# A recurrent attention and its MLP on one core: chunk gates on VectorE, a second chunk of exponents on TensorE, paired weight tails, three early blocks and a planner that knows of a shared port

## The chip, the cores and the metric

The kernel runs on one core of a Trainium2 chip. The metric is device microseconds of one execution. The core has TensorE (PE; its weight loads are shown as PEld), VectorE (DVE), ScalarE (ACT), GpSimd (POOL) and SyncE (SP), whose queue issues the DMAs. Each engine works through its own instructions in order.

## The reference, cut to what matters

Two stages follow each other. The first is an mLSTM: for 4 batches and 8 heads, over 768 steps, with head size 40:

```
m_new = max(f[t] + m, i[t])
C = exp(f[t] + m - m_new) * C + exp(i[t] - m_new) * outer(v[t], k[t])
n = exp(f[t] + m - m_new) * n + exp(i[t] - m_new) * k[t]
y[t] = sigmoid(o[t]) * (C q[t]) / max(|n.q[t]|, 1)
```

The 3072 rows of 320 values then go through an MLP: `h = x @ w_in` (320 by 2048), `g = h * erf(softplus(h))`, `out = g @ w_out` (2048 by 320). The weights arrive as 64-bit floats.

## The kernel before, in words

**Attention.** The recurrence is computed in 6 chunks of 128 steps (`NC`), for 4 batches, so there are 24 attention steps; step `s` is chunk `s // 4`, batch `s % 4`. Within a chunk all heads are done as masked matrix products: `S` (L581) multiplies k and q, `w` (L596) multiplies that with the decay matrix `dm`, `ph` (L614 to L623) forms outputs and the state's update, `sk` and `sa` (L633 to L648) keep the state, `yg`, `y` and `yy` (L654 to L668) finish a row, `tr` (L674) turns it, and `xh`, `xl` (L688, L692) store it in a high and a low part for the MLP.

**Decays.** `dm` is an exponent of cumulative gate sums with a causal mask. In chunk 0 TensorE forms the argument (`pe`, L523 to L526) from sums split into three bf16 parts, with the mask added by a product; `ex` (L535) takes the exponent from PSUM. In chunks 1 to 5 the row sums are read back from DRAM as a broadcast over all partitions (`bq`, L543, 512 KB), GpSimd adds the column part (`add`, L555), ScalarE takes the exponent (L559), and GpSimd applies the mask (`sel`, L564). The gate sums of chunk 0 are made alone (`gload` to `split`, L370 to L402). Those of all chunks are then made in one set of instructions over 768 columns on 32 partitions (`lload` to `lrest`, L416 to L450), partly on VectorE (two scans, L422 and L445) and partly on GpSimd (L428 to L437, L450), and written to DRAM (L459).

**Weights.** Twenty-two pieces of raw 64-bit weights (`win`, `tail`, `wout`) are loaded and decoded in the kernel by `decode` (L699): `val` on ScalarE (L707), `dec`, two instructions on VectorE (L712, L713), `hi` on ScalarE (L718) and `lo` on GpSimd or VectorE (L724). The last 64 rows of w_in, the tail, are loaded twice per quarter of the columns so that the high part stands in one half of the partitions and the low part in the other.

**MLP.** Two attention steps make a block of 256 rows; there are 12 blocks. A phase is half a block's MLP: `up` (L807, 64 matmuls a phase), a copy `hb` (L816 on ScalarE or L818 on VectorE), softplus `sp` (L826), `er` (L830), `mu` (L834), `gh` and `gl`, the high and low parts (L839, L844), and `dn` (L869 to L872). Softplus, erf and exp each need a table load on ScalarE.

**Order.** `Plan` (L51) orders everything. Each step is a part with an engine, a cost in microseconds, predecessors, buffers from counted slots and, for some, a due time (`target`). `issue` places parts one by one at the earliest possible time and prefers the one that is due first, shifted by a hand-kept table (`NUDGE`). The engines' queues come out of that plan. `CHAIN` fixes the order of exponents, softplus and erf on ScalarE. `ORDER` (L264) fixes the order of the phases: first halves of blocks 0 and 1, then their second halves, and then block after block. First halves need half of w_in and half of w_out. From step `CLUSTER` on, `tr`, `S` and `ph` of three steps are merged into one TensorE part. `SLOTS` and `CAPS` count buffers.

Of the kernel before, what the change touches and what calls it, by code (L numbers as in the profile page):

```python
# [9 lines left out]
F32 = mybir.dt.float32  # L10
# [8 lines left out]
L = 128  # L19
# [10 lines left out]
NB = 2  # L30
# [20 lines left out]
class Plan:  # L51
# [13 lines left out]
    def add(self, engine, cost, fn, after=(), new=(), use=(), target=None, kb=0.0, table=None, mode=0, order=()):  # L65
# [8 lines left out]
        p.into, p.leaves = None, mode  # L74
        self.parts.append(p)
        return p
# [18 lines left out]
    def issue(self):  # L95
# [34 lines left out]
        table, mode, dma = None, 0, 0.0  # L130
# [3 lines left out]
        def can(p):  # L134
            t = max(free[p.engine], p.ready)
            for b in p.new:
                for tag in b.tags:
                    s = slots[tag]
                    need = sum(tag in x.tags for x in p.new) + (KEEP.get(b.tag, 0) if tag == 'big' else 0)
                    if len(s) < need:  # L140
                        return None
                    t = max(t, sorted(s)[need - 1][0])
            return t + 2 * self.TABLE * (p.table is not None and len(p.table) > 1 and table not in p.table)

        while len(out) < len(parts):
            best = None
            for e, rs in ready.items():
                ts = [(t, p) for p in rs if (t := can(p)) is not None]
                if not ts:
                    continue  # L150
                first = min(t for t, _ in ts)
                cost = lambda p: PREFER * self.ENTER.get((mode, p.mode), 0.0) if e == 'PE' else 0.0
                _, _, t, p = min((p.late + cost(p), p.n, t, p) for t, p in ts if t <= first + 0.02)
# [13 lines left out]
            free[p.engine] = end  # L167
            if p.engine == 'SP':
# [832 lines left out]
```

## Time and profile before

| | |
|---|---|
| median of 3 runs | 493.35 us (491.83 to 493.83) |
| the profiled execution's own time | 493.03 us |
| its span, first to last instruction | 491.2 us |
| busy: PE, DVE, ACT, POOL | 449.3, 344.1, 332.6, 175.3 us |
| mean granted TensorE clock | 0.961 |
| moved by DMA | 53.75 MB |

A page of the profile gives the span in 40 slices, a digit for each engine's busy tenths, and the clock that TensorE was granted (`PEclk`). Other views of the same trace are the busy time of each engine in stretches that one chooses, the waits (who waited for whom: total, times, longest), groups of instructions by line (count, then busy total and mean ns of one, then idle time before them), a timeline (start, length, engine, line) and the chain of waits that ended last (start, length, what). Busy time of VectorE and GpSimd includes time in which an instruction has started and cannot go on.

### The profile page before, as it was taken

What the parts mean: (1) busy time and instruction counts of PE and PEld (TensorE: products, weight loads), DVE (VectorE), ACT (ScalarE), POOL (GpSimd) and SP (SyncE); (2) the same over time, 40 slices, a digit from 0 to 9 for tenths busy, and PEclk for the clock granted to TensorE, in tenths of its full rate; (3) what the DMA queues carried; (4) which work ended last, traced back from release to release, by engine and by line L of the source; (5) the groups of instructions that cost most, each with busy time, mean ns of one, the idle gap of its engine ahead of it and who ended that gap; (6) DMA issues with size and microseconds to landing.
All of it is one profiled execution on the core that took longest, in us unless ns stands there. A gap on an engine that the chain in (4) does not pass through costs nothing.

```text
span 491.2 us, 13646 instructions
## 1 busy us (share of the span) xinstructions
PE 449.3 (91%) x6013; PEld 433.4 (88%) x6013; DVE 344.1 (70%) x493; ACT 332.6 (68%) x383; POOL 175.3 (36%) x150
## 2 busy tenths in 40 slices
PE   1696863997999999999999999999999999999997
PEld 0476852986999999999999999999999999999997
DVE  2779798999849458659849658767766854755561
ACT  3554888487775569958967847757668667366691
POOL 6439476657537134223303503403403510200000
PEclk9967988798899999999999999999999999999999
DMA  8978858430553325314505314323333300000000
GB/s 245 239 243 252 259 162 259 136 90 11 152 150 95 103 65 161 109 32 136 166 4 160 120 48 136 119 77 107 119 116 85 102 3 28 1 28 2 1 27 29
DMA packets 31164, 53.75 MB, mean 109 GB/s; under 512 B 3200, under 2 KB 19840, under 8 KB 31104
## 3 DMA queue, kind: packets, MB, share of 16 engines
q1 hardware_dynamic: 31104, 52.87, 36.9%
q8 instruction: 47, 0.77, 0.7%
q14 instruction: 13, 0.11, 0.1%
HBM read 48.73 MB, written 4.13 MB: 108 GB/s over the span
## 4 chain that ended last, share of the span: by engine, by line
PE 76%; DMA 10%; DVE 8%; ACT 3%; issue 2%; POOL 1%; SPq 1%; DVEq 0%; ACTq 0%; POOLq 0%
PE h L807 32%; PE po L869 11%; PE po L872 11%; PE po L870 11%; DMA raw<-in_w_in_dram 4%; PE pa L581 4%; PE pa L614 3%; DMA raw<-in_w_out_dram 3%; DVE bits L713 3%; PE pa L618 2%; DMA dq<-dec_dr 2%; PE pa L674 1%; DVE bits L712 1%; DVE gl L844 1%; PE pa L623 1%
## 5 line engine op out<-in xcount | busy, mean ns | idle before, releaser
L807 PE MATMUL h<-xh,wh 128*128 128x256 f32 x576 | 158.3, 285 | 1.3 <-DVE hb L818 0.9
L807 PE MATMUL h<-xl,wh 128*128 128x256 f32 x576 | 157.5, 283 | 1.6 <-DVE xl L692 1.6
L869 PE MATMUL po<-woh,gh 128*128 128x320 f32 x384 | 118.7, 321 | 9.6 <-ACT o_sb L890 8.1
L870 PE MATMUL po<-wol,gh 128*128 128x320 f32 x384 | 116.2, 314 | 1.7 <-POOL wol L724 1.7
L807 PEld LDWEIGHTS h<-xh,wh 128*128 128x128 f32 x576 | 109.6, 190 | 2.3 <-DVE hb L818 1.4
L807 PEld LDWEIGHTS h<-xl,wh 128*128 128x128 f32 x576 | 109.7, 190 | 1.8 <-DVE xl L692 1.8
L807 PE MATMUL h<-xh,wl 128*128 128x256 f32 x384 | 109.1, 284 | 2.2 <-POOL wl L724 2.2
L662 POOL TENSOR_TENSOR kvo<-kvo,den 128x320 f32<-128x320 f32 x24 | 25.3, 1052 | 179.4 <-DVE kvo L658 179.4
L818 DVE COPY hb<-h 128x512 f32<-128x512 f32 x84 | 57.6, 686 | 41.4 <-PE h L807 40.8
L826 ACT ACTIVATE e<-hb 128x1024 f32<-128x1024 f32 x48 | 50.6, 1059 | 52.6 <-DVE hb L818 52.4
L869 PEld LDWEIGHTS po<-woh,gh 128*128 128x128 f32 x384 | 74.0, 193 | 11.1 <-ACT o_sb L890 8.3
L870 PEld LDWEIGHTS po<-wol,gh 128*128 128x128 f32 x384 | 74.1, 193 | 1.9 <-POOL wol L724 1.9
L834 DVE TENSOR_TENSOR hb<-e,hb 128x1024 f32<-128x1024 f32 x48 | 65.4, 1372 | 14.6 <-ACT e L830 14.6
L807 PEld LDWEIGHTS h<-xh,wl 128*128 128x128 f32 x384 | 73.1, 190 | 2.4 <-POOL wl L724 2.4
L872 PE MATMUL po<-woh,gl 128*128 128x320 f32 x384 | 73.3, 313 | 1.3 <-DVE gl L844 1.3
L844 DVE TENSOR_TENSOR gl<-hb,gh 128x1024 fp32r<-128x1024 f32 x44 | 63.1, 1435 | 5.5 <-ACT gh L839 5.1
L839 ACT ACTIVATE gh<-hb 128x1024 fp32r<-128x1024 f32 x48 | 50.3, 1054 | 20.2 <-DVE hb L834 19.9
L872 PEld LDWEIGHTS po<-woh,gl 128*128 128x128 f32 x384 | 61.5, 192 | 1.6 <-DVE gl L844 1.5
L555 POOL TENSOR_TENSOR dm<-dm,aT 128x1024 f32<-128x1024 f32 x20 | 48.2, 2409 | 18.3 <-DMA dm<-cum_dr 18.3
L830 ACT ACTIVATE e<-e 128x1024 f32<-128x1024 f32 x48 | 49.3, 1054 | 0.3
L654 DVE TENSOR_SCALAR den<-pa 128x8 f32<-128x8 f32 x24 | 3.9, 165 | 55.2 <-PE pa L623 41.8
L826 ACT ACT_TABLE_LOAD x28 | 35.9, 1283 | 4.1 <-DVE hb L818 3.6
(91 smaller groups left out, 646.3 us busy)
## 6 DMA issues: line engine op xcount, KB each, us to landing
dm<-cum_dr SPq DMA_DIRECT2D x20, 512.0 KB
qk<-in_qk_dram SPq DMA_DIRECT2D x24, 416.0 KB
kvo<-in_kvo_dram SPq DMA_DIRECT2D x24, 324.0 KB
raw<-in_w_in_dram SPq DMA_DIRECT2D x8, 512.0 KB
kvo<-in_kvo_dram SPq DMA_DIRECT2D x24, 160.0 KB
out_dram<-o_sb SPq DMA_DIRECT2D x24, 160.0 KB
raw<-in_w_out_dram SPq DMA_DIRECT2D x8, 320.0 KB
dq<-dec_dr SPq DMA_DIRECT2D x20, 128.0 KB
```

The source lines that it names most:

```text
L555: nc.gpsimd.tensor_tensor(v.dm, v.dm, aT[:, c - 1, 8 * b:8 * b + 8].unsqueeze(2).to_broadcast([128, H, L]), op=ALU.add)
L662: nc.gpsimd.tensor_tensor(v.y[:, 0:DM].rearrange("p (h d) -> p h d", d=D), v.th.rearrange("p (h d) -> p h d", d=D), v.den.unsqueeze(2).to_ ...
L807: nc.tensor.matmul(V.h[i][:, n % 2 * T:(n % 2 + 1) * T], w, m, start=(q == 0), stop=(q == len(ops) - 1))
L818: nc.vector.tensor_copy(V.hb[:, i * 512:(i + 1) * 512], V.h[i])
L826: nc.scalar.activation(V.e, V.hb, AF.Softplus)
L830: nc.scalar.activation(V.e, V.e, AF.Erf)
L834: nc.vector.tensor_tensor(V.hb, V.e, V.hb, op=ALU.mult)
L839: nc.scalar.activation(V.gh, V.hb, AF.Copy)
L844: (nc.gpsimd if f in GL_POOL else nc.vector).tensor_tensor(V.gl, V.hb, V.gh.bitcast(F32), op=ALU.subtract)
L869: nc.tensor.matmul(K.po[b], V.gh[:, ts], woh[:, w], start=start, stop=False)
L870: nc.tensor.matmul(K.po[b], V.gh[:, ts], wol[:, w], start=False, stop=False)
L872: nc.tensor.matmul(K.po[b], V.gl[:, ts], woh[:, w], start=False, stop=stop)
```

## The change

The diff is long, since the planner's tables (`CHAIN`, `NUDGE`, the sets that choose an engine) are replaced as a whole. Its parts:

- **Second chunk by TensorE.** `pe`, `rows` and the two `ex` are used for chunks 0 and 1 (`if c < 2`); `bq`, `add` and `sel` remain for chunks 2 to 5.
- **Gate sums per chunk.** `gate_chunk(c)` takes the place of both sets of gate instructions. All sums are on VectorE; the maximum is carried from chunk to chunk; sums go to DRAM in four small writes a chunk. `late`, `lg`, `lones`, `lrest` are gone.
- **Tails in pairs.** One `val` and one `dec` serve two quarters of the columns; each quarter keeps its `hi` and `lo`.
- **Three early blocks.** `EARLY = 3`, so the phases begin (0,0), (1,0), (2,0), (0,1), (1,1), (2,1).
- **The shared port in the plan.** Parts with `lock`, and all of GpSimd's, are placed one after another on a common `port` time. The costs of many parts are set anew (`add` from 2.7 to 1.95, `sel` from 1.4 to 1.15, `gl` on GpSimd from 2.8 to 2.42).
- **Engine choices.** `GL_POOL` is empty, so every `gl` is on VectorE. `y` and `yy` of steps 0 and 1 go to VectorE. `hb` of phase 4 goes from ScalarE to VectorE. `vg` of steps 1 and 3 goes to VectorE, that of step 4 to GpSimd. `lo` is on VectorE for i31, o5, o8, o9 in place of o1, o6, t0. `hi` is on VectorE for i01 and o5. `lo` of i01 is formed by two TensorE products and a ScalarE copy; `LO_PE` also lists t0, t2 and t3, but `weights_tail` no longer calls `decode`, where that set is looked up.
- **Buffers.** `dm`, `xh`, `xl`, the outputs and chunk 0's constants move into the common slots (`big`, 19 to 26).
- **Loads.** The q and k loads of steps 13 and later follow the issue of all w_out loads (`AFTER`).

```
-    def add(self, engine, cost, fn, after=(), ..., mode=0, order=()):
+    def add(self, engine, cost, fn, after=(), ..., mode=0, order=(), lock=False):
+        p.into, p.leaves, p.lock = None, mode, lock or engine == 'POOL'
...
+                    t = max(at, p.ready, port if p.lock else 0.0)
...
+            if p.lock:
+                port = end
...
+SLOTS = dict(pa=4, h=2, po0=1, po1=1, big=26, vg=2, dq=2, bits=2, den=2, gt=1, m_c=2, x0=2, aT=2, spl=1)
+EARLY = 3
+HB_ACT = {0, 6}
+HI_DVE = {'i01', 'o5'}
+LO_DVE = {'i31', 'o5', 'o8', 'o9'}
+LO_PE = {'i01', 't0', 't2', 't3'}
+GL_POOL = set()
+CLUSTER = 9
+AFTER = 13
+VG_POOL = {0, 2, 4, 6, 7}
+Y_DVE = {0, 1}
+ORDER = [(k, hh) for hh in range(2) for k in range(EARLY)] + [(k, hh) for k in range(EARLY, NK) for hh in range(2)]
...
+        @make(f'sum{c}', 'DVE', 1.05, after=[scan], new=[x0b], use=[gtb, m_b], lock=True)
+        def total():
+            v.x = x = new(sb, [128, 3, L], F32, "x0")
+            nc.vector.tensor_tensor(x[:, Y], v.gt[:, 1], v.m[:, 0:L], op=ALU.add)
+            nc.vector.tensor_tensor(x[:, Y], x[:, Y], v.m[:, 1:L + 1], op=ALU.subtract)
+            if c == 0:
+                nc.vector.memset(x[:, Y, 0:1], 0.0)
+            nc.vector.tensor_tensor_scan(out=x[:, C], data0=x[:, Y], data1=zero.to_broadcast([128, L]), initial=0.0,
+                                         op0=ALU.add, op1=ALU.add)
...
+        def kept(name, t, i, after):
+            @make(f'{name}{c}', 'SP', 1.4, kb=16.0, after=after, use=[x0b])
+            def put():
+                for b in range(B):
+                    nc.sync.dma_start(t[c, b], v.x[32 * b:32 * b + H, i])
...
-        if c == 0:
+        if c < 2:
             peb = [Buf('pa') for _ in range(2)]
...
+            def rest():
+                v.lo = new(ps, [128, 512], F32, "pa")
+                nc.tensor.matmul(v.lo, ident, v.val, start=True, stop=False)
+                nc.tensor.matmul(v.lo, minus, hi(), start=False, stop=True)
...
+        for v_ in step[AFTER:]:
+            v_.load.order.append(load)
```

More of the change, by code (lines that the diff above doesn't have):

```diff
@@ L63, in __init__, with add @@
         self.parts, self.slots = [], dict(slots)
-    def add(self, engine, cost, fn, after=(), new=(), use=(), target=None, kb=0.0, table=None, mode=0, order=()):
+    def add(self, engine, cost, fn, after=(), new=(), use=(), target=None, kb=0.0, table=None, mode=0, order=(), lock=False):
         p = Part()
@@ L129, in issue @@
         free = {e: 0.0 for e in self.LAG}
-        table, mode, dma = None, 0, 0.0
+        table, mode, dma, port = None, 0, 0.0, 0.0
         ready = {e: [p for p in parts if p.engine == e and not p.wait] for e in self.LAG}
         out = []
-        def can(p):
-            t = max(free[p.engine], p.ready)
+        for p in parts:
+            p.needs = {}
             for b in p.new:
                 for tag in b.tags:
-                    s = slots[tag]
                     need = sum(tag in x.tags for x in p.new) + (KEEP.get(b.tag, 0) if tag == 'big' else 0)
[L140 to L143, printed above, removed]
+                    p.needs[tag] = max(need, p.needs.get(tag, 0))
+            p.needs = [(slots[tag], need) for tag, need in p.needs.items()]
+            p.slow = p.table is not None and len(p.table) > 1
         while len(out) < len(parts):
@@ L385, in total @@
-    @make('sum', 'DVE', 0.6, after=[g, p_small], use=[firstb])
-    def total():
-        nc.vector.tensor_tensor_scan(out=first.x[:, 1], data0=first.y, data1=zero.to_broadcast([128, L]), initial=0.0,
-                                     op0=ALU.add, op1=ALU.add)
-    @make('rest', 'POOL', 0.9, after=[total], use=[firstb])
-    def rest():
-        x = first.x[:, 0]
-        nc.gpsimd.tensor_tensor(x, first.gt[:, 0], first.m[:, 1:L + 1], op=ALU.subtract)
-        nc.gpsimd.tensor_tensor(x, x, first.x[:, 1], op=ALU.subtract)
@@ L396, in split @@
-    @make('split', 'DVE', 2.1, after=[rest, p_cst], use=[firstb])
-    def split():
-        x, spl = first.x, first.spl
-        for m in (nm1, nm2):
-            nc.vector.tensor_copy(spl, x)
-            nc.vector.scalar_tensor_tensor(out=x, in0=spl, scalar=m, in1=x, op0=ALU.mult, op1=ALU.add)
-        nc.vector.tensor_scalar(out=spl, in0=x, scalar1=pm, scalar2=pa, op0=ALU.mult, op1=ALU.add)
-    late = SimpleNamespace()
-    R = B * H
-    gib, gfb, gmb, gyb, gcb = (Buf('late') for _ in range(5))
@@ L408, in row @@
-    def row(name):
-        return big(name)[0:R]
-    @make('lload', 'SP', 1.2, kb=200.0, new=[gib, gfb])
-    def lload():
-        late.i, late.f = row("late"), row("late")
-        for b in range(B):
-            for t, x in ((late.i, 0), (late.f, 1)):
-                nc.sync.dma_start(t[8 * b:8 * b + 8, 0:S], gates[32 * b:32 * b + 8, x])
-    @make('lscan', 'DVE', 3.2, after=[lload, p_small], new=[gmb], use=[gib, gfb])
-    def lscan():
-        late.m = row("late")
-        nc.vector.tensor_copy(late.m[:, 0:1], m0[0:R])
-        nc.vector.tensor_tensor_scan(out=late.m[:, 1:S + 1], data0=late.f[:, 0:S], data1=late.i[:, 0:S], initial=m0[0:R],
-                                     op0=ALU.add, op1=ALU.max)
@@ L440, in tile_mlstm_moe @@
-    p_lones = reset(gyb)
-    @make('lsum', 'DVE', 3.2, after=[lg, p_lones], new=[gcb], use=[gfb, gyb])
-    def lsum():
-        late.c = row("late")
-        nc.vector.tensor_tensor_scan(out=late.c[:, 0:S], data0=late.one[:, 0:S], data1=late.f[:, 0:S], initial=0.0,
-                                     op0=ALU.mult, op1=ALU.add)
-    @make('lrest', 'POOL', 2.0, after=[lsum], use=[gib, gcb])
-    def lrest():
-        nc.gpsimd.tensor_tensor(late.i[:, 0:S], late.i[:, 0:S], late.c[:, 0:S], op=ALU.subtract)
@@ L452, in gexp @@
-    @make('gexp', 'ACT', 0.85, after=[lsum], use=[gcb, gfb], table=('exp',))
-    def gexp():
-        nc.scalar.activation(late.f[:, 0:S], late.c[:, 0:S], AF.Exp)
-    def kept(name, t, src, after, buf):
-        @make(name, 'SP', 0.5, kb=100.0, after=after, use=[buf])
-        def put():
-            nc.sync.dma_start(t.rearrange("c b h l -> (b h) c l"), src()[:, 0:S].rearrange("p (c l) -> p c l", l=L))
-        return put
-    p_cum = kept('cumw', cum_dr, lambda: late.c, [lsum], gcb)
-    p_dec = kept('decw', dec_dr, lambda: late.f, [gexp], gfb)
@@ L506, in loadv, with dqp @@
             v.y = n[:, 0:DM + 64]
+        if c > 0:
+            @make(f'dq{s}', 'SP', 0.9, after=[G.dec], kb=208.0, new=[dqb])
+            def dqp():
+                v.dq = new(sb, [128, NPR, L], F32, "dq")
+                for j in range(2):
+                    n = 64 if j == 0 else D
+                    nc.sync.dma_start(v.dq[64 * j:64 * j + n],
+                                      dec_dr[c, b:b + 1].rearrange("o (p j) l -> o j p l", j=2)[:, j].to_broadcast([n, NPR, L]))
         ex, sel = [], []
-        if c == 0:
+        if c < 2:
             peb = [Buf('pa') for _ in range(2)]
-            @make(f'rows{s}', 'POOL', 0.5, after=[split, p_zeros], use=[firstb])
+            @make(f'rows{s}', 'POOL', 0.45, after=[G.split, p_zeros], use=[G.splb, earlyb], order=prev.pe if c else [])
             def rowsp():
-                nc.gpsimd.tensor_copy(splB[b][rows], first.spl[rows])
-            @make(f'pe{s}', 'PE', 1.35, after=[rowsp, p_ones, p_mask], new=peb, use=[maskb], target=due - 14, mode=3,
+                nc.gpsimd.tensor_copy(early.spl[b][rows], G.spl[rows])
+            @make(f'pe{s}', 'PE', 1.45, after=[rowsp, p_ones, p_mask], new=peb, use=[maskb, earlyb], target=due - 14, mode=3,
                   order=[step[s - 1].S] if s > 0 else [])
@@ L560, in attention @@
             ex.append(e)
-            @make(f'sel{s}', 'POOL', 1.4, after=[e], use=[dmb])
+            @make(f'sel{s}', 'POOL', 1.15, after=[e], use=[dmb])
             def sl():
@@ L585, in attention @@
         if not last:
-            @make(f'vg{s}', *(('POOL', 1.0) if s in VG_POOL else ('DVE', 0.47)), after=[*sel, loadv], new=[vgb], use=[dmb, kvb])
+            @make(f'vg{s}', *(('POOL', 0.8) if s in VG_POOL else ('DVE', 0.52)), after=[*sel, loadv], new=[vgb], use=[dmb, kvb], lock=True)
             def vgp():
@@ L707, in val @@
             nc.scalar.activation(v.val, raw().bitcast(F32)[:, :, 1], AF.Prelu, scale=REBIAS, alpha=NEGATIVE)
-        @make(f'dec{name}', 'DVE', 1.4, after=[val], use=[vb, rawb])
+        @make(f'dec{name}', 'DVE', 1.18, after=[val], use=[vb, rawb], lock=True)
         def bits():
@@ L742, in weights_in, with weights_tail @@
         win[part].append(decode(f'i{part}{k}', lambda: pair(v.raw), b, [load], lambda: wh[:, k, cs], lambda: wl[:, k, cs]))
-    def weights_tail(part):
+    def weights_tail(pair_):
         v = SimpleNamespace()
-        b = Buf('raw')
-        @make(f'tail{part}', 'SP', 1.0, kb=512.0, new=[b])
+        b, vb = Buf('raw'), Buf('bits')
+        cols = [slice(part * 512, (part + 1) * 512) for part in (2 * pair_, 2 * pair_ + 1)]
+        at = [slice(0, 64), slice(64, 128)]
+        @make(f'tail{pair_}', 'SP', 1.0, kb=512.0, new=[b])
         def load():
@@ L751, in load, with val, bits, high @@
             for i in range(2):
-                nc.sync.dma_start(v.raw[64 * i:64 * i + 64], w_in.bitcast(I32)[256:320, part * 1024:(part + 1) * 1024])
-        cs = slice(part * 512, (part + 1) * 512)
-        win[part].append(decode(f't{part}', lambda: pair(v.raw), b, [load], lambda: wh[:, 2, cs], None))
+                nc.sync.dma_start(v.raw[at[i]], w_in.bitcast(I32)[256:320, 2 * cols[i].start:2 * cols[i].stop])
+        @make(f'valt{pair_}', 'ACT', 0.7, after=[load], new=[vb], use=[b], table=('exp', 'er'))
+        def val():
+            v.val = new(sb, [128, 512], F32, "bits")
+            nc.scalar.activation(v.val, pair(v.raw).bitcast(F32)[:, :, 1], AF.Prelu, scale=REBIAS, alpha=NEGATIVE)
+        @make(f'dect{pair_}', 'DVE', 1.18, after=[val], use=[vb, b], lock=True)
+        def bits():
+            t = v.val.bitcast(I32)
+            nc.vector.tensor_scalar(out=t, in0=t, scalar1=3, scalar2=None, op0=ALU.logical_shift_left)
+            nc.vector.scalar_tensor_tensor(out=t, in0=pair(v.raw)[:, :, 0], scalar=29, in1=t,
+                                           op0=ALU.logical_shift_right, op1=ALU.bitwise_or)
+        for i in range(2):
+            name = f't{2 * pair_ + i}'
+            engine = 'DVE' if name in LO_DVE else 'POOL'
+            @make(f'hi{name}', *(('DVE', 0.36) if name in HI_DVE else ('ACT', 0.64)), after=[bits], use=[vb], lock=name in HI_DVE)
+            def high(i=i, on_dve=name in HI_DVE):
+                w = wh[at[i], 2, cols[i]]
+                if on_dve:
+                    nc.vector.tensor_copy(w, v.val[at[i]])
+                else:
+                    nc.scalar.activation(w, v.val[at[i]], AF.Copy)
+            @make(f'lo{name}', engine, dict(DVE=0.72, POOL=1.3)[engine], after=[high], use=[vb], lock=True)
+            def low(i=i, e=nc.vector if engine == 'DVE' else nc.gpsimd):
+                e.tensor_tensor(wh[at[1 - i], 2, cols[i]], v.val[at[i]], wh.bitcast(F32)[at[i], 2, cols[i]], op=ALU.subtract)
+            win[2 * pair_ + i].append(low)
     def weights_out(u):
@@ L839, in ghp @@
                 nc.scalar.activation(V.gh, V.hb, AF.Copy)
-            @make(f'gl{f}', *(('POOL', 2.8) if f in GL_POOL else ('DVE', 1.24)), after=[ghp], new=[gl], use=[hb, gh])
+            @make(f'gl{f}', *(('POOL', 2.42) if f in GL_POOL else ('DVE', 1.25)), after=[ghp], new=[gl], use=[hb, gh], lock=True)
             def glp(V=V):
```

260 lines of the change are left out of this document (143 added, 117 removed), and 102 rows, old and new, of tables (CHAIN, NUDGE).

## The prediction

> **What bounds the kernel now.** I read the 40 slices first, then busy time by stages, then TensorE's waits, then the instructions inside the bad stages.
>
> ```profile
> PE   1696863997999999999999999999999999999997
> PEclk9967988798899999999999999999999999999999
> ```
>
> From slice 12 on TensorE has no gap and a full clock; what can be won lies in the first 11 slices (12.28 us each) and the end of the last. Stages cut at the first matmul (10.30), the first `up` matmul (35.65), the middle of the decode (92) and the point where `ph` and `S` of steps 6 and 7 end the ramp (135.4). The columns are the stage and its length, then busy time and instructions of PE, PEld, DVE, ACT and POOL, then granted clock, DMA share and GB/s:
>
> ```profile
> 0.00:10.30 10.30, 0.00 (x0) 0.00 (x0) 3.03 (x8) 3.52 (x5) 7.02 (x26) 1.00 0.77 220
> 10.30:35.65 25.35, 19.96 (x406) 14.21 (x406) 16.80 (x31) 13.30 (x28) 10.49 (x14) 0.80 0.89 243
> 35.65:92.00 56.35, 37.84 (x325) 35.69 (x325) 50.17 (x56) 39.15 (x54) 38.88 (x24) 0.82 0.77 231
> 92.00:135.40 43.40, 38.87 (x640) 36.96 (x639) 39.94 (x53) 31.44 (x38) 26.56 (x19) 0.92 0.31 88
> 135.40:442.00 306.60, 306.60 (x4306) 300.75 (x4305) 210.93 (x324) 215.37 (x230) 92.31 (x69) 1.00 0.31 91
> 442.00:491.20 49.20, 46.08 (x344) 45.81 (x342) 23.18 (x25) 29.83 (x31) 0.00 (x0) 1.00 0.04 15
> ```
>
> TensorE idles 10.3, 5.4 (25.35 less 19.96), 18.5, 4.5, 0 and 3.1 us in these six stages. The 3.1 are the last copy and store. Busy time at a low clock adds an estimated 20% of 19.96, 18% of 37.84 and 8% of 38.87: 4.0 + 6.8 + 3.1 = 13.9 us. So 491.2 is about 435 us of TensorE work at full clock and 56 us lost, of which some 33 us (18.5 + 4.5 + 6.8 + 3.1) lie between 35.65 and 135.4. There VectorE is busy 89% and then 92%, more than ScalarE and GpSimd. What TensorE waits for in that stretch:
>
> ```profile
> PE po L869 <- ACT o_sb L890: 8.1, 1, 8.1
> PE pa L581 <- DVE dm L596: 2.9, 1, 2.9
> PE h L807 <- POOL wl L724: 2.2, 1, 2.2
> PE pa L618 <- DVE dm L596: 1.8, 1, 1.8
> ```
> ```profile
> 85.75 0.64 PE L869 MATMUL po<-woh,gh 128*128 128x320 f32 x1 [8.12 <-ACT o_sb L890]
> ```
>
> One wait of 8.1, and small ones behind VectorE and GpSimd that sum, with the rest of the 23.0, to 14.9. The 8.1 carries ScalarE's name, but the second fence, a row of TensorE's timeline, puts it at 77.6 to 85.75, after both early first halves of `up` and one early `dn`: TensorE has nothing else to do, since the second halves want weights still being decoded. Why are VectorE and GpSimd so late?
>
> ```profile
> 88.92 0.69 DVE L713 SCALAR_TENSOR_TENSOR bits<-raw,bits 128x512 int32<-128x512 int32 x1
> ...
> 90.13 0.42 DVE L712 TENSOR_SCALAR bits<-bits 128x512 int32<-128x512 int32 x1
> 90.58 1.66 DVE L713 SCALAR_TENSOR_TENSOR bits<-raw,bits 128x512 int32<-128x512 int32 x1
> ...
> 92.76 1.21 DVE L844 TENSOR_TENSOR gl<-hb,gh 128x1024 fp32r<-128x1024 f32 x1
> ```
> ```profile
> 90.41 1.27 POOL L724 TENSOR_TENSOR wl<-bits,wh 128x512 fp32r<-128x512 f32 x1 [1.82 <-ACT wh L718]
> ```
>
> The same L713 takes 0.69 alone and 1.66 when GpSimd's L724 runs from 90.41 to 91.68: it ends at 92.24, 0.56 after GpSimd. The two do not share, one waits out the other. The price up to 125 us:
>
> ```profile
> L713 DVE SCALAR_TENSOR_TENSOR bits<-raw,bits 128x512 int32<-128x512 int32 x22 | 26.5, 1205 | 0.8
> L712 DVE TENSOR_SCALAR bits<-bits 128x512 int32<-128x512 int32 x22 | 16.5, 752 | 6.6 <-ACT bits L707 6.6
> L818 DVE COPY hb<-h 128x512 f32<-128x512 f32 x12 | 8.2, 683 | 2.3 <-PE h L807 2.3
> L844 DVE TENSOR_TENSOR gl<-hb,gh 128x1024 fp32r<-128x1024 f32 x4 | 8.1, 2032 | 0.0
> ```
>
> Against 22 x 0.69, 22 x 0.42 and 4 x 1.21 that is 11.3 + 7.3 + 3.3 = 21.9 us of waiting counted as VectorE's busy time. **The ramp is bound by VectorE and GpSimd taking turns.**
>
> **The change, part by part.** The rows of GpSimd's work that goes, up to 125 us:
>
> ```profile
> L555 POOL TENSOR_TENSOR dm<-dm,aT 128x1024 f32<-128x1024 f32 x4 | 8.8, 2211 | 0.0
> ...
> L844 POOL TENSOR_TENSOR gl<-hb,gh 128x1024 fp32r<-128x1024 f32 x2 | 5.2, 2590 | 0.0
> ...
> L564 POOL TENSOR_SCALAR_AFFINE_SELECT dm<-dm 128x1024 f32<-128x1024 f32 x3 | 3.5, 1180 | 7.5 <-ACT dm L559 7.5
> ...
> L428 POOL TENSOR_TENSOR late<-late 32x768 f32<-32x768 f32 x1 | 1.9, 1890 | 0.1
> L429 POOL TENSOR_TENSOR late<-late 32x768 f32<-32x768 f32 x1 | 1.9, 1872 | 0.1
> ```
>
> (1) *GpSimd's relief.* Chunk 1's `add` and `sel` go (8.8 + 3.5), the late gate sums (1.9 + 1.9, and L430 and L450 over the same shape, taken as 3.3 together), and `gl` of the early phases (5.2): 24.6 us of the 65.4 that GpSimd is busy between 35.65 and 135.4, or 38%. `y` of two steps and two of the lows (`i31`, `o5`/`o8`/`o9` in place of `o1`/`o6`/`t0`) move off too, four `rows` of chunk 1 come on; these I let cancel. SP's queue loses chunk 1's four broadcasts (`bq`), the eight row loads of the late gates and four of the eight tail loads; it gains 36 small writes of chunk sums, most of them after 100 us. None of these issues is among TensorE's waits above.
>
> (2) *VectorE's account.* It gains `gl` (2 x 1.21 early), a second `split` (below, the first begins at 7.68 and the matmul behind it at 10.30, so under 2.6; I take 2.1), the sums of chunks 0 to 3, and `hb` of one phase. A gate chunk is two scans (0.48 and 0.42) and four two-input sums of 128x128 that no row shows: between nothing and the 0.42 of a scan of that size; I take 0.25, so 1.9 a chunk, 7.6 for four. The old 768-wide scans go:
>
> ```profile
> L422 DVE TENSOR_TENSOR_SCAN late<-late,m 32x768 f32<-32x768 f32 x1 | 2.9, 2904 | 0.0
> ```
>
> The paired tails keep their highs and lows and drop two `val` and two `dec`, which saves 2 x (0.42 + 0.69) = 2.2 here. In all about +2.4 + 2.1 + 7.6 + 2.7 (four `hb` like L818's 0.68) - 2.9 - 2.2 = +9.7 clean, and 38% of 21.9 = -8.3 of waiting. VectorE's busy time in the ramp hardly falls. What improves is its order and what TensorE has in hand meanwhile.
>
> (3) *The start.*
>
> ```profile
> 5.97 0.42 DVE L387 TENSOR_TENSOR_SCAN late<-late,zero 128x128 f32<-128x128 f32 x1 [2.00 <-POOL late L383]
> 7.68 0.29 DVE L400 CAST late<-late 128x256 bf16<-128x256 f32 x1 [1.29 <-POOL late L394]
> ```
>
> Two hand-overs to GpSimd (3.3 us of waiting) become four sums on VectorE itself (1.0): up to 2.3 us earlier. The first `up` also waits for DMA (89% busy from 10.30 to 35.65), so I take -1, with 0 and -2 as bounds.
>
> (4) *Third early block.* One more phase of `up`, 64 matmuls, needs only the first half of w_in and is ready in the place of the 8.1 wait. Two pieces of the chain of waits show what such matmuls take, after a wait (0.20 each) and late in the span at full clock (0.12 each):
>
> ```profile
> 45.40 6.13 PE h L807 x30
> ```
> ```profile
> 455.59 7.59 PE h L807 x64
> ```
>
> 7.6 us would nearly fill it. But block 2 needs steps 4 and 5, so I take -6.5 (bounds 0 and -8.1). The second halves and half of w_out are wanted a phase later.
>
> (5) *The other waits* (14.9): GpSimd's 38%, and an order that knows of the turns: -6.5 (0 to -12).
>
> (6) *Clock.* The slow stretches follow the waits: of 6.8 + 3.1 about half, -4.5 (0 to -8).
> The Trainium skill (TensorE: Matmul & The Clock Gate, "What's actually happening") gives about 3.4 us of idleness before the clock falls. By that only the wait of 8.1 costs clock, about 1.7 us, and the sum would come out 2.8 us higher. The trace disagrees: the slow stretch at 45.40 comes after a wait of 2.2 us.
>
> (7) *TensorE's added work.* The exponents of four steps, 4 x what one takes now:
>
> ```profile
> 14.07 0.39 PE L523 MATMUL pa<-rhsE,splB 128*128 128x512 bf16 x1
> 14.30 0.39 PE L525 MATMUL pa<-splB,rhsE 128*128 128x128 bf16 x4
> ```
>
> A step issues six such groups, 0.23 apart (14.07 to 14.30): 1.4, and 5.6 for four. The low part of `i01` is two f32 matmuls over 512 columns that no row shows: from twice the 0.23 of a bf16 one over 512 to four times that, 0.5 to 1.8; I take 1.0. Of 6.6 I put half on the path, +3 (0 if all of it falls into waits, +6.6 if none does).
>
> (8) *The steady stretch* stays at nothing: VectorE works 210.93 of 306.60 there, GpSimd 92.31, and the new chunk sums add 1.9 per four steps. Covered by that slack; without it, the second rival.
>
> Sum: -1 - 6.5 - 6.5 - 4.5 + 3 = -15.5, so 491.2 becomes 475.7. The profiled execution took 493.03, 1.83 over its span, and lies 0.3 below the median of 493.35. Predicted: 475.7 + 1.8 = 477.5.
>
> **The rivals.** *VectorE stays the bound.* By (2) its work does not shrink; 89% and 92% leave no room. Then the third block gives half its worth, the small waits and the clock stay: -1 - 3 - 1 - 1 + 2 = -4, some 489. For it: the ledger. Against: work that the first halves don't need is put off.
>
> *Slower: late chunk sums.* Before, one set of instructions made all later sums. Now each of chunks 2 to 5 goes through scans on VectorE's in-order queue, a write, a read, `add`, exp, `sel`; behind the write's wait on the one DMA queue stand the next loads of q, k and v. One broadcast took this long:
>
> ```profile
> 53.77 9.02 DMA dq<-dec_dr
> ```
>
> 1.9 + 9 + 2.2 for `add` and 1.2 for `sel` (the means of their rows) are 14.3, with the exponent some 15 us a chunk. If the order leaves half of it uncovered, 4 x 7.5 = 30 is lost: 477.5 + 30 = 507. From 3.9 uncovered a chunk the gain is gone. Against it: a full TensorE phase of cover, and the slack in (8).
>
> *TensorE never starves after the first `up`.* All of 18.5 + 4.5 + 9.9 and the start's 2 won, 6.6 paid: -28, so 465. For it: GpSimd's relief and the put-off decodes together exceed the waits. Against: a queue order planned from costs has left 23 us of waits in this trace.
>
> *The change does nothing:* the order that comes out trades one wait for another, 493.
>
> **How the numbers follow.** Forecast (471 to 484) 0.55, VectorE bound 0.16, never starves 0.16, nothing 0.05, late sums 0.08. A measurement of this kernel can tell about 0.5%, 2.5 us. Faster: 0.55 + 0.16 + 0.12 of the VectorE case = 0.83; same: 0.04 + 0.04 = 0.08; slower 0.09 (0.08 and 0.01 of the nothing case). The range takes in the VectorE case and most of the third rival: 465 to 490.
>
> **What would show it.** First matmul near 8.5 instead of 10.30; no wait of 8 us around 80, `up` of block 2 in its place; L713's line nearer to 0.9 than to 1.2 us; `add` 16 times instead of 20; TensorE without a gap from 115 to 125 on instead of 122. Wrong: VectorE over 90% busy with the waits unchanged, or waits on `dm` or `aT` at chunk borders after 150 us.

## The result, and the profile after

The changed kernel takes 481.69 us (median of four runs, 481.31 to 489.12) against 493.59 for the kernel before beside it; the ratio is 0.9761 with a 95% interval of 0.9727 to 0.9795. The run of 489.12, with a mean clock of 0.972, is not in the ratio. The profiled execution took 481.77, with a span of 480.1 and a clock of 0.989. The forecast was 477.5 (465 to 490).

The engines' busy time and two of the 40-slice strips:

```profile
PE 448.1 (93%) x6057; PEld 430.9 (90%) x6063; DVE 333.4 (69%) x550; ACT 331.7 (69%) x388; POOL 119.1 (25%) x121
...
PE   2695988999798999999999999999999999999997
...
PEclk9999998999999999999999999999999999999999
```

Before, slices 4 to 7 had 6, 8, 6 and 3 tenths of TensorE's work; now they have 5, 9, 8 and 8, and slices 11 and 13 have small dents. The clock falls below 0.9 in one slice only. GpSimd fell from 175.3 to 119.1 us. Stages cut at the first matmul, the first `up`, and then 92, 145 and 434 (columns as in the prediction's table):

```profile
0.00:8.77 8.77, 0.00 (x1) 0.01 (x1) 4.15 (x13) 3.95 (x6) 4.40 (x17) 1.00 0.73 220
8.77:29.97 21.20, 17.34 (x391) 11.96 (x393) 13.40 (x30) 12.32 (x26) 6.51 (x8) 0.92 1.01 301
29.97:92.00 62.03, 50.85 (x708) 47.08 (x703) 50.65 (x94) 43.21 (x66) 25.67 (x25) 0.94 0.68 200
92.00:145.00 53.00, 50.27 (x643) 48.31 (x644) 41.93 (x63) 46.48 (x52) 11.94 (x10) 1.00 0.20 57
145.00:434.00 289.00, 286.77 (x4012) 280.90 (x4013) 203.57 (x332) 197.43 (x214) 70.58 (x63) 1.00 0.30 92
434.00:480.10 46.10, 42.90 (x316) 42.63 (x314) 19.67 (x21) 28.35 (x28) 0.00 (x0) 0.99 0.04 15
```

TensorE idles 8.8, 3.9, 11.2, 2.7, 2.2 and 3.2 us: 32.0 in all, 41.9 before. Busy time at a low clock is 17.34 x 0.08 + 50.85 x 0.06 = 4.4 us, 13.9 before. What is left, 443.7, is work at full clock, 435.4 before. So the span fell by 11.1 = 9.9 (idle) + 9.5 (clock) - 8.3 (more work). VectorE is busy 82% and 79% of the two stages from 29.97 to 145, no longer 89% and 92% of the stages of the ramp. What TensorE waits for now:

```profile
PE pa L532 <- POOL early L523: 9.2, 2, 8.8
PE pa L619 <- issue: 5.7, 3, 2.5
PE pa L677 <- POOL kvo L671: 5.0, 1, 5.0
PE po L920 <- issue: 2.2, 1, 2.2
PE h L855 <- issue: 2.1, 1, 2.1
PE po L918 <- issue: 1.2, 1, 1.2
```

The wait of 8.1 and those behind `wl`, `wol` and `gl` are gone. Two kinds stand in their place. One `tr` (L677) waits 5.0. And in six waits the profile names no releaser ("issue"): 5.7 + 2.2 + 2.1 + 1.2 = 11.2 us. The kernel before had one:

```profile
PE pa L618 <- issue: 3.5, 1, 3.5
```

The decode on VectorE up to 145 us (the paired tails' two pieces, on a line of their own, had no waiting):

```profile
L715 DVE SCALAR_TENSOR_TENSOR bits<-raw,bits 128x512 int32<-128x512 int32 x18 | 14.6, 810 | 0.6
...
L892 DVE TENSOR_TENSOR gl<-hb,gh 128x1024 fp32r<-128x1024 f32 x10 | 12.2, 1218 | 2.2 <-ACT gh L887 2.1
...
L714 DVE TENSOR_SCALAR bits<-bits 128x512 int32<-128x512 int32 x18 | 10.0, 557 | 5.5 <-ACT bits L709 5.4
```

Against 0.69, 1.21 and 0.42 alone, that is 2.2 + 0.1 + 2.5 = 4.8 us of waiting behind GpSimd in place of 21.9.

Where did the old gap of 77.6 to 85.75 go? Two rows of TensorE's timeline:

```profile
75.64 0.56 PE L920 MATMUL po<-woh,gl 128*128 128x320 f32 x2 [2.19 <-issue]
```
```profile
87.06 0.36 PE L855 MATMUL h<-xh,wh 128*128 128x256 f32 x1
```

From 75.64 to 86.53 TensorE works on `dn` of the first two phases. `up` of the third early block starts only at 87.06, behind the old gap. In the kernel before, `dn` stood still in this gap: it was `dn` that became ready sooner, and not the third block that filled it. The reason stands in ScalarE's timeline, first before, then after:

```profile
85.28 0.42 ACT L890 ACTIVATE o_sb<-po 128x320 f32<-128x320 f32 x1
```
```profile
76.24 0.44 ACT L937 ACTIVATE o<-po 128x320 f32<-128x320 f32 x1 [4.62 <-PE po L920]
```

TensorE could start the next block's `dn` only when ScalarE had copied the finished output out of its place in PSUM. Before, that output was finished by 76.5, but ScalarE worked with hardly a pause from 77.65 on (the second erf, a table load, an exponent, decoding, both `gh`) and reached the copy at 85.28. Now both `gh` are done by 71.6, and it is ScalarE that waits, 4.62 us, for TensorE.

### The profile page after: what moved, and what is told of

Its sections match the earlier page's. It is cut to its first block, busy times and chain, and to the rows that moved or that the text cites. A ratio compares the mean times of both kernels' runs of the same rounds, so it can differ in the third digit from the quotient of the medians.

```text
span 480.1 us, 13788 instructions
## 1 busy us (share of the span) xinstructions
PE 448.1 (93%) x6057; PEld 430.9 (90%) x6063; DVE 333.4 (69%) x550; ACT 331.7 (69%) x388; POOL 119.1 (25%) x121
## 4 chain that ended last, share of the span: by engine, by line
PE 86%; DVE 4%; issue 4%; ACT 2%; DMA 2%; SPq 0%; POOL 0%; DVEq 0%; ACTq 0%; POOLq 0%
PE h L855 35%; PE po L917 12%; PE po L920 12%; PE po L918 12%; PE pa L582 5%; PE pa L619 3%; PE pa L615 3%; PE pa L677 2%; PE pa L624 1%; DMA qk<-in_qk_dram 1%; DMA cst<-in_consts_dram 1%; PE pa L532 1%; DVE bits L715 1%; DVE bits L714 1%; DVE dm L597 1%
## 5 line engine op out<-in xcount | busy, mean ns | idle before, releaser
L918 PE MATMUL po<-wol,gh 128*128 128x320 f32 x384 | 114.9, 311 | 1.2 <-issue 1.2
L866 DVE COPY hb<-h 128x512 f32<-128x512 f32 x88 | 60.2, 688 | 53.3 <-PE h L855 52.0
L918 PEld LDWEIGHTS po<-wol,gh 128*128 128x128 f32 x384 | 72.9, 190 | 1.6 <-issue 1.5
L917 PEld LDWEIGHTS po<-woh,gh 128*128 128x128 f32 x384 | 72.9, 190 | 1.3
L665 POOL TENSOR_TENSOR kvo<-kvo,den 128x320 f32<-128x320 f32 x22 | 21.6, 980 | 181.6 <-DVE kvo L659 167.8
L892 DVE TENSOR_TENSOR gl<-hb,gh 128x1024 fp32r<-128x1024 f32 x48 | 59.5, 1246 | 5.2 <-ACT gh L887 4.9
L556 POOL TENSOR_TENSOR dm<-dm,aT 128x1024 f32<-128x1024 f32 x16 | 32.1, 2015 | 29.3 <-DVE aT L463 28.4
```

Of the source, the lines that this page charges most:

```text
L556: nc.gpsimd.tensor_tensor(v.dm, v.dm, G.aT[:, b].unsqueeze(2).to_broadcast([128, H, L]), op=ALU.add)
L866: nc.vector.tensor_copy(V.hb[:, i * 512:(i + 1) * 512], V.h[i])
L892: (nc.gpsimd if f in GL_POOL else nc.vector).tensor_tensor(V.gl, V.hb, V.gh.bitcast(F32), op=ALU.subtract)
L917: nc.tensor.matmul(K.po[b], V.gh[:, ts], woh[:, w], start=start, stop=False)
L918: nc.tensor.matmul(K.po[b], V.gh[:, ts], wol[:, w], start=False, stop=False)
```

## The experiments

The theory to test: the ramp got faster since GpSimd's work that held VectorE up was taken away and the third early block fills the wait. The rivals: the order (the plan that knows of the port) did it, or the exponents of chunk 1. And two new waits wanted a cause. Every ratio is to the kernel before on the same chip in the same hour.

**Waits without a releaser.** All six lie in `ph` or shortly behind it; `ph` issues 128 matmuls and as many loads in some 1.7 us. TensorE's matmuls from the start to just before four of these waits (x counts them):

```profile
0.00:22.50 22.50, 9.98 (x220) 0.99 0.91 256
0.00:70.20 70.20, 48.65 (x853) 0.95 0.80 234
...
0.00:128.90 128.90, 102.45 (x1488) 0.96 0.58 174
0.00:148.20 148.20, 120.55 (x1744) 0.97 0.56 165
```

Divided by 128 these leave 92, 85, 80 and 80. With a load for each matmul, 128 matmuls are 256 instructions. The Trainium skill (Runtime: NRT & Kernel Launch, "Instruction fetch mechanics") says that instructions are fetched in blocks of 16 KiB, 256 of them, and that crossing a border is mostly hidden. The page of the profile agrees on the size, 16 KB a packet; that the crossing is mostly hidden does not hold for these 11.2 us.

```profile
q8 instruction: 47, 0.77, 0.7%
```

The trace also has the time of each packet of that queue. Beside the six waits they are:

| TensorE idle, us | packet under way, us |
|---|---|
| 20.07 to 22.55 | 20.10 to 21.18 |
| 68.08 to 70.27 | 67.36 to 68.69 |
| 73.45 to 75.64 | 73.27 to 74.16 |
| 126.90 to 128.99 | 126.59 to 127.55 |
| 147.08 to 148.29 | 145.89 to 146.84 |
| 154.57 to 155.59 | 152.96 to 154.19 |

Each wait ends 1.4 to 1.6 us after its packet has landed. Over the traces of both kernels and all experiments, 60 of the 61 waits without a releaser (above 0.15 us) end 1.2 to 1.7 us after such a packet, and only 5 of the 156 waits that have a releaser. So TensorE stands there until its next block of instructions has come. Four kernels move the borders or thin out `ph`:

```
 # after, one: 64 / two: 128 / five: 32 small f32 products ahead of the first pe
+for _ in range(64):
+    nc.tensor.matmul(t[0:32, 0, 0:41], ident[:, 0:32], ident[:, 0:41], ...)
 # three: ph of steps 4 and 5 in one piece, 56 matmuls in place of 128 each
-quarters = [slice(32 * i, 32 * i + 32) for i in range(4)]
+quarters = [slice(0, 128)] if s in (4, 5) else [slice(32 * i, 32 * i + 32) for i in range(4)]
```

> The changed kernel with 64 more small matmuls (ident by ident, 128 instructions with their loads, their result overwritten) ahead of the first one, in TensorE's first wait; nothing else moves. In the changed kernel six waits of TensorE carry no releaser (2.48, 2.19, 2.19, 2.09, 1.21 and 1.02 us, 11.2 in all); counted in matmuls from the first they lie at 229, 870, 998, 1518, 1778 and 1906, and with a load for each matmul 870 to 998 and 1778 to 1906 are 256 instructions each. Theory (instructions are fetched in blocks of 256, and a block comes late): the waits move 64 matmuls earlier in the kernel's own work, that is they keep their counts if the added ones are counted too: 870 falls inside the ph of step 4 instead of that of step 5, 998 into that of step 5 or the end of it, 1906 before the ph it cuts now. Time within 3 us of 481.7. Rival (a wait on a semaphore or a transfer that the profile does not show): they stay before the same instructions, at 934, 1062, 1842 and 1970 with the added ones counted.

Measured: 483.23, span 481.5 (one run). Four of the six waits stood at the same instructions as before, at 71.37, 76.19 (0.29 us alone), 127.86 and 149.27. What I expected of it was worked out wrongly: an f32 product is recorded as two matmuls with two loads, so 64 products are a whole block and the borders fall where they fell.

> As with 64, but 128 more matmuls, one whole block of 256 instructions. Theory: the waits are before the same instructions of the kernel's own work as in the changed kernel (counts 357, 998, 1126, 1646, 1906, 2034 with the added ones), lengths within 0.7 us. The rival says the same here; together with the 64 it tells a block boundary from a place that moves with any change. Time within 2 us of 481.7; the first matmuls find a faster clock if the added ones end shortly before them, at most 1.4 us less.

Measured: 482.59, span 480.9 (one run). Two whole blocks, and again the same instructions wait (25.32, 72.71, 78.08, 129.33, 148.63, 156.39), three of them 0.8 to 1.8 us shorter, where I had expected 0.7 at most. This and the first fit the theory of blocks, but the rival expected the same of whole blocks.

> The changed kernel with the ph of steps 4 and 5 issued in full width (128 rows at once instead of four times 32): 56 matmuls instead of 128 a step, same result. Theory (late instruction blocks): the waits of 2.19 in ph and in dn at 70 and 75 us go or shrink to under 1.5 together, since the two ph now take 224 instructions instead of 512; TensorE's own work may rise by 0 to 1.5 us a step. Time 477 to 481. Rival (unseen wait): both waits stay at 2.2, and the time is 481.7 plus the added work, 482 to 485.

Measured: 479.91 (477.43 to 481.70), ratio 0.9733 (0.9681 to 0.9785). TensorE's waits without a releaser:

```profile
PE pa L619 <- issue: 2.2, 1, 2.2
PE pa L624 <- issue: 1.5, 1, 1.5
```

3.7 us instead of 11.2; both waits of 2.19 behind `ph` of step 5 are gone. The reading that fits: `ph`, now some 3 us with 112 instructions, uses a block up more slowly. The price is 5.7 us more of TensorE's work at full clock, where I had expected 3 at most, so the gain over the changed kernel is not measurable (the intervals overlap).

> The changed kernel with 32 small f32 products ahead of TensorE's first matmul. The runs with 64 and 128 showed that the trace records each f32 product as two matmuls, so those were shifts by a whole block and by two, and their waits without a releaser came at the same instructions as in the changed kernel; 32 are 64 matmuls with 64 loads, half a block of 256. Matmuls counted exactly up to each such wait give, modulo 128: changed kernel 92, 85, 85, 80, 80, 78; with 64: 89, 89, 86, 86; with 128: 95, 94, 89, 89, 87, 86, 84. Theory (blocks of 256 instructions come late): the same remainder, 78 to 96, with the 64 added ones counted, so the waits are 64 matmuls earlier in the kernel's own work: around 68 us inside the ph of step 4 after about half of it, not in that of step 5 after 10 of its 128; another may open or close. Rival (an unseen semaphore or transfer): the waits stay at the same instructions, remainder 14 to 32. Time within 3 us of 481.7.

Measured: 502.26, span 500.6 (one run): the same work, 20 us more. TensorE's waits, and its matmul count just before some of them:

```profile
PE po L921 <- issue: 8.7, 3, 3.0
...
PE pa L627 <- issue: 3.7, 2, 1.9
PE pa L618 <- issue: 3.1, 1, 3.1
PE po L923 <- issue: 3.1, 1, 3.1
```
```profile
0.00:229.50 229.50, 207.12 (x3026) 0.95 0.51 150
0.00:250.30 250.30, 226.08 (x3282) 0.95 0.49 145
...
0.00:333.40 333.40, 301.19 (x4306) 0.94 0.45 131
0.00:354.20 354.20, 318.96 (x4562) 0.95 0.44 129
```

All four counts leave 82, and so do those of the two between them (3794 and 4050). In the steady stretch, where the changed kernel has none, TensorE now stops 1.8 to 3.1 us at every second to fourth border. After 160 us idle time rises from 3.2 to 18.8 and the loss at a low clock (busy time by one less the clock, summed over stretches of 1 us) from 0 to 6.2. So the waits belong to counts of instructions and not to data. The packets that end these six waits started late: TensorE then had 0, 46, 0, 3, 0 and 0 matmuls left to the border.

The clock fell at 229.64, 287.67 and 311.56, so at three of the six waits; at the two longest, 3.05 and 3.08, it did not. In all these traces it changes only at points that lie 3.41 us or a multiple of that apart. TensorE had idled 2.8, 1.8 and 2.0 us of the 3.41 before the three falls, and at most 1.7 of any such stretch around the other three waits.

The same half block in front of the kernel before:

> The kernel before, with 32 small products (64 matmul records, half a block of 256 instructions with their weight loads) in front of TensorE's first real one; the same work otherwise. Theory of blocks: the steady stretch of the kernel before has the same sequence of instructions as that of the kernel after, where half a block cost 20 us; so TensorE gets waits without a releaser here too, of 1 to 3 us each behind a ph, at remainders of 78 to 95 of the count of matmuls by 128, and the time is 503 to 515. Rival, that the loss belongs to the order of the kernel after alone: 491 to 496, with no wait of this kind behind 150 us.

Measured: 494.28, span 492.3 (one run), with one wait without a releaser (2.7, at 28.2) and none behind 150 us. The rival held. Half a block is bad for the order of the changed kernel, not for every order; the borders do not explain the difference between the two kernels. `ph` begins at like counts in both steady stretches (remainders of the matmul count 67 to 105 before, 72 to 89 in the shifted one), so a like place of the border is not enough. The packets differ: here those of the steady stretch start 45 to 148 matmuls ahead of their border, by the same count, and land at least 4 us before TensorE reaches it. What decides when a block is asked for stays open.

**GpSimd's relief alone.** In the kernel before, with its order kept, the sums of chunk 1's `dm`, the late gate sums and every `gl` go from GpSimd to VectorE:

```
-nc.gpsimd.tensor_tensor(f, f, m[:, 0:S], op=ALU.add)
+nc.vector.tensor_tensor(f, f, m[:, 0:S], op=ALU.add)
...
-nc.gpsimd.tensor_tensor(v.dm, v.dm, aT[...], op=ALU.add)
+(nc.vector if c == 1 else nc.gpsimd).tensor_tensor(v.dm, v.dm, aT[...], op=ALU.add)
...
-(nc.gpsimd if f in GL_POOL else nc.vector).tensor_tensor(V.gl, V.hb, V.gh...)
+nc.vector.tensor_tensor(V.gl, V.hb, V.gh...)
```

> The kernel before, its order kept, with three kinds of work taken from GpSimd to VectorE: gl of phases 2 and 4, the late gate sums (lg, lrest), and add of chunk 1. GpSimd loses some 21 us of busy time up to 140 us, VectorE gains some 11 clean. Theory (most of the gain is GpSimd's relief, as the plan without the port suggested, 484.6): the mean of the decode's second instruction falls from 1.20 to 1.0 or less, TensorE's waits between 35 and 135 us fall by 4 to 9 us, time 484 to 489. Rival (the third early block and the new order carry the gain): VectorE's added work cancels it, time 491 to 495.

Measured: 488.75 (484.65 to 490.52), ratio 0.9904 (0.9870 to 0.9937): 4.6 us of the 11.9. One group on VectorE and TensorE's largest wait inside the ramp:

```profile
L713 DVE SCALAR_TENSOR_TENSOR bits<-raw,bits 128x512 int32<-128x512 int32 x22 | 21.8, 992 | 0.8
```
```profile
PE po L869 <- ACT o_sb L890: 6.8, 1, 6.8
```

The decode gets faster (0.99 instead of 1.21), the wait on `dn` shrinks by 1.3 and stays, the clock does not recover (14.3 us lost, 14.2 before, over stretches of 1 us). GpSimd's busy time over the whole span fell by 28.9 us (175.3 to 146.4), and not by the 56.2 of the change, and VectorE took the work over. So the relief is real and brings at least this much; what all of it would bring in the old order was not measured. The wait on `dn` again ends with ScalarE's copy, at 84.44: VectorE's relief alone does not close that gap.

**The plan's knowledge of the port.** The changed kernel, planned without a common port time:

```
-p.into, p.leaves, p.lock = None, mode, lock or engine == 'POOL'
+p.into, p.leaves, p.lock = None, mode, False
```

> The changed kernel planned without the common port time: the order of all queues comes out anew, work and engines stay. Theory (the order is what took VectorE's waiting from 21.9 to about 5 us in the ramp): the mean of the decode's second instruction on VectorE (0.81 us now, 1.20 before, 0.69 alone) rises over 1.0, TensorE's waits grow, time 485 to 492. Rival (taking work off GpSimd was enough): mean under 0.9 and time within 3 us of 481.7. Caution: the table of nudges was made for the plan with the port, so a loss can also be that.

Measured: 484.56 (483.70 to 488.78), ratio 0.9843 (0.9792 to 0.9893), by the medians 2.9 us slower than with it (the intervals touch). VectorE's L715 took 0.74 us, less than the 0.81 of the changed kernel, so the plan's knowledge of the port is not what frees VectorE. The order as such may have a part: with the old order and part of the relief the mean stayed at 0.99, and in the four new orders (the changed kernel's, this one and two more below) it is 0.69 to 0.86. What a new search of the order would bring with the work of the kernel before was not tried. The hand-kept shifts were made for the plan with the port, so the 2.9 may overstate that knowledge.

**The 5.0 of `tr`.** GpSimd's timeline in the changed kernel:

```profile
39.75 0.73 POOL L665 TENSOR_TENSOR kvo<-kvo,den 128x320 f32<-128x320 f32 x1
44.41 1.37 POOL L742 TENSOR_TENSOR wol<-bits,woh 128x512 fp32r<-128x512 f32 x1 [3.93 <-ACT woh L723]
45.73 0.23 POOL L671 COPY kvo<-kvo 128x64 f32<-128x64 f32 x1
```

The copy of 0.23 that `tr` needs stands behind a `lo`, which waits 3.93 for ScalarE. I moved seven parts forward in the finished order:

```
+move('y3', 'yg3'); move('yy3', 'y3'); move('rows4', 'split1')
+move('tr3', 'tr2'); move('xh3', 'xh2'); move('xl2', 'xh3'); move('xl3', 'xl2')
```

> The changed kernel with seven parts of block 1 moved forward in the written order (y3 and yy3 behind yg3, tr3 behind tr2, xh3 behind xh2, xl2 and xl3 behind it, rows4 behind split1), no work changed. The wait of 5.04 us at 41 to 46 us is for yy3, which stands in GpSimd's queue behind a low that waits for ScalarE; the plan put y3 there because it holds GpSimd back while VectorE splits, and the trace shows y3 running beside the split. Theory (the wait is lost time that the plan's port model made): it goes or shrinks below 1.5 us, up of block 1 starts by 46 instead of 49, and time falls by 2 to 5 us, 477 to 480. Rival (what follows is bound by decode on VectorE anyway): the wait goes and returns before dn or up of block 2, time within 1.5 us of 481.7.

Measured: 484.39 (482.93 to 486.62), ratio 0.9816 (0.9771 to 0.9861): no gain, by the medians 2.7 us slower than the changed kernel (the intervals overlap). The wait of `tr` went and this came:

```profile
PE pa L619 <- issue: 7.9, 3, 3.1
PE h L855 <- DVE hb L866: 6.4, 2, 6.3
```

The theory that this wait was TensorE's to win fell: behind it stood a wait for VectorE's `hb`, longer than itself. Waits without a releaser come to 11.6, as good as unchanged.

**TensorE's added work.** The low part of i01 by VectorE in place of the two TensorE products:

```
-nc.tensor.matmul(v.lo, ident, v.val, start=True, stop=False)
-nc.tensor.matmul(v.lo, minus, hi(), start=False, stop=True)
-nc.scalar.activation((lo or hi)()[h], v.lo[h], AF.Copy)
+nc.vector.tensor_tensor((lo or hi)()[h], v.val[h], hi().bitcast(F32)[h], op=ALU.subtract)
```

> The changed kernel with the low part of i01 made by one subtraction on VectorE instead of two TensorE products and a ScalarE copy, at the same place of the written order. Theory (TensorE's added work is paid in full now that TensorE hardly waits): the four matmul records of 23.4 to 25.8 us go, time falls by 1 to 2.5 us, 479 to 480.7. Rival (it lies in a wait): time within 0.7 us of 481.7.

Measured: 481.48 (481.14 to 483.01), ratio 0.9773 (0.9739 to 0.9807): no difference. In the one trace, TensorE's work at full clock fell by 0.9 us and idle time by 1.4 (waits without a releaser came to 8.5), while the loss at a low clock rose by 1.7. Two new small waits:

```profile
PE pa L677 <- DVE kvo L671: 0.9, 1, 0.9
PE pa L677 <- ACT state L645: 0.8, 1, 0.8
```

**The third early block.** `EARLY = 2`, with the hand-kept shifts searched anew, since the plan depends on them:

> The kernel after with two early blocks in place of three, its order searched anew (planned span 470.3 against 466.5). Theory, that the third early block is what filled the 8.1 us wait: a wait of 5 to 9 us of an up quarter of a fresh block comes back between 60 and 95 us, and the time is 487 to 491. Rival, that a wait at this place can be filled by other work once VectorE no longer stands behind GpSimd: no wait above 4 us between 60 and 95, and the time is 480 to 484.

Measured: 476.58 (475.99 to 477.53), ratio 0.9674 (0.9636 to 0.9711): faster than the changed kernel, and the fastest of all. No wait above 1 us lies between 60 and 95. The first product of `up` for a second half (the 129th of all), and the waits:

```profile
64.45 0.39 PE L810 MATMUL h<-xh,wh 128*128 128x256 f32 x1
```
```profile
PE pa L632 <- POOL kvo L626: 5.7, 1, 5.7
...
PE pa L579 <- issue: 1.0, 1, 1.0
...
PE h L810 <- issue: 0.9, 1, 0.9
```

In the kernel before, that product started at 91.96. Here the second half of w_in begins to be ready by 64, and there is no gap for a third block. Of its lead over the changed kernel, waits without a releaser are 8.5 us (2.7 instead of 11.2); the other idle time is 2.7 more (26.2 - 2.7 against 32.0 - 11.2). So between these two orders the third block goes with 2.7 us fewer waits for data, and the two-block order owes its lead to shorter waits for blocks of instructions, which the plan doesn't know of: it had this order 3.8 us slower. Whether three blocks in an order with as few of these waits would be as fast wasn't tried.

**Chunk 1's exponents.** The changed kernel with `bq`, `add`, `sel` for chunk 1 (`if c < 1` in place of `if c < 2`), searched anew:

> The kernel after with chunk 1's exponents by the old way (the broadcast load, the sum of 1.7 us on GpSimd, exponent and masking), its order searched anew (planned span 478.9). TensorE is given back the four pe products (5.7 us). Theory, that TensorE's gain is smaller than what VectorE and GpSimd lose in the ramp (four sums of 1.7 us and four maskings there, beside which VectorE's decode runs at 1.2 us and not 0.8): VectorE's decode mean rises to 0.95 or more, waits of 8 to 14 us come in, and the time is 484 to 490. Rival, that the gate sums alone were the relief and the exponents cost as much as they bring: 478 to 483, with TensorE's idle time within 3 us of that of the kernel after.

Measured: 501.85 (500.46 to 503.15), ratio 1.0184 (1.0143 to 1.0226): 20 us slower than the changed kernel and slower than before, beyond what either expected. The decode's mean is 0.86 us, hardly more than 0.81; the port is not the cause. The waits:

```profile
PE h L809 <- ACT xh L644: 6.9, 1, 6.9
...
PE pa L569 <- DVE dm L551: 3.6, 1, 3.6
PE po L871 <- ACT gh L841: 3.0, 1, 3.0
```

Idle time is 13.8 us higher, the loss at a low clock 9.2 higher and TensorE's work 4.7 lower: 18.4 of span. `ph` waits for `dm`, and `up` for a block that is not stored. The plan itself had 12.4 us more (478.9 against 466.5), so a good part is that this order is worse, and its search may have been the poorer one. Shown is that this order without the four products is worse; how much the exponents are worth in the best order for each stays open.

**Both small edits.** The thin `ph` of steps 4 and 5 with the low part on VectorE:

> The kernel after with ph of steps 4 and 5 at full width (fewer and wider products, as in an earlier run) and the low part of i01 by VectorE in place of TensorE's two products (as in another). Theory, that both act on different waits and add up: 477 to 480. Rival, that the waits of tr and S that the second brought in eat its 2.4 us and that blocks fall otherwise: 480 to 483.

Measured: 479.65 (478.00 to 481.42), ratio 0.9728 (0.9692 to 0.9765), the same as the thin `ph` alone. That lies in the range of the theory, but the two gains did not add up: the second edit adds nothing here either.

## Why the prediction was right, and which terms were mis-sized

**Start** (-1): first matmul at 8.77, not 10.30: -1.5. Right.

**Third early block** (-6.5): the wait of 8.1 went, so the number came near by luck, but the step failed: "ready in the place of the 8.1 wait" named the wrong filler. `up` of block 2 came at 87.06, after the place; `dn` filled it, and with two early blocks the gap does not come back. The sign that I named, `up` of block 2 in its place, was not seen. The reading of the wait had failed before it: I passed over ScalarE's name and looked to weights still being decoded, while TensorE's `dn` waited for ScalarE's copy.

**GpSimd's relief and VectorE's ledger**: right in kind; VectorE's waiting fell by 17.1 us (21.9 to 4.8) where I took 8.3. I had scaled it with GpSimd's busy time; the partial relief in the kernel before alone brought some 10 (22 x 0.30 + 22 x 0.15 + 8 x 0.24 = 11.8 left). What brought the rest, of more relief, pairs and the new order, was not taken apart.

**Other waits** (-6.5): idle time behind the first matmul, without the 8.1 and without waits that name no releaser, fell from 41.9 - 10.3 - 8.1 - 3.5 - 3.1 = 16.9 to 32.0 - 8.8 - 11.2 - 3.2 = 8.8, so -8.1. But waits without a releaser grew from 3.5 to 11.2, +7.7, and the net is -0.4. That term was missing: I had no term for the one of 3.5 and had not asked where it came from.

**Clock** (-4.5): -9.5, mis-sized. I had counted the two middle stages alone (6.8 + 3.1) and given them half. They fell to 3.1, and the stage ahead of the first `up`, which I had left out, from 4.0 to 1.4. I weighed there a rule of the Trainium skill (TensorE: Matmul & The Clock Gate, "What's actually happening") by which the clock falls after some 3.4 us of idleness. The shifted kernel, which lost 6.2 us of clock behind 160 us with no wait above 3.1 us, speaks against it as the row at 45.40 did, though there the clock fell at 43.75, inside that wait and shortly behind one of 1.8.

**TensorE's added work** (+3): +8.3, all of it in the span. Three of the four `pe` took 1.48, near the 1.4 forecast, and one 2.70 at half clock. The two low products took 2.4 us, nearly all of it at half clock (0.50 from 22.14 to 25.55), so an estimated 1.3 at full clock where I took 1.0. That makes some 7 of the 8.3; the rest I can't place. The step that failed is "half on the path": the work was not hidden in waits. But taking the low products away bought nothing, as a larger loss at a low clock stood against it.

**Steady stretch** (nothing): right. From 145 to 434 TensorE idles 2.2 us, and both waits in it (1.2 and 1.0) are without a releaser; the chunk sums hold up nobody, and that rival fell. `add` ran 16 times. Another sign failed: TensorE was to have no gap from 115 to 125 us on, and three waits for blocks of instructions come after, the last up to 155.59. The sum of the terms is -1.5 - 8.1 - 8.1 + 7.7 - 9.5 + 8.3 = -11.2, against 11.1 measured. That the forecast of -15.5 lay only 4.4 from it is in part luck: two errors of some 5 us, the clock and the added work, cancel, and the missing term of 7.7 was in part made up by the other waits, which fell by more than I took.

## What to carry to other kernels

Before filling a gap with extra work, ask what ends it, and take the engine's name that the profile gives seriously: here it was ScalarE's queue, VectorE's relief alone left 6.8 of the 8.1, and in the new orders the gap was gone, with three early blocks as with two. When TensorE works 93% of a span, added matmuls are hardly hidden (8.3 us more of work, all of it in the span), and stretches of many short matmuls can stop at fixed counts of instructions: look for a packet of the instruction queue in front of each wait that names no releaser, and time a version with some harmless instructions ahead before trusting a gain of 2%. A new plan per edit moves the time by several us on its own, so undo parts in the finished order where that can be done.

## What the hardware showed unexpectedly

That time hangs on where a program's instructions are counted from: half a block of extra instructions, run while TensorE had nothing to do, cost 20 us, and a whole block or two cost nothing that these single runs show (483.23 and 482.59 against 481.69). And short waits can cost clock as well: in the shifted kernel's steady stretch 15.6 us of added idleness (18.8 less 3.2) brought 6.2 us more at a low clock. What counts is not the length of the wait alone, but how much of it falls between two of the points 3.41 us apart at which the clock can change. Over all these traces, the clock fell behind every such stretch at full clock in which TensorE had idled more than 1.85 us (46 of 46, the start and the last 8 us left out), and 53 of its 55 falls followed at least 1.69 us.
